# Linear attention and a token/channel mixer on one core: the first batch by halves of the heads, weight loads in another form, attention steps in other slots

## The chip, the core and the metric

The kernel runs on one core of one Trainium2 chip. A core has a matrix engine (TensorE, PE in the profile; PEld is its weight load), a vector engine (VectorE, DVE), an activation engine (ScalarE, ACT), GpSimd (POOL), and SyncE (SP), which here only issues transfers. DVE and ACT read and write both the on-chip memory SBUF and the accumulators of TensorE, PSUM (eight banks of 512 f32 columns for each of 128 partitions); POOL reads and writes SBUF alone. Transfers between HBM and SBUF, and transposes from SBUF to SBUF, are carried by 16 DMA engines. They are issued from SP, ACT or POOL; each issuing engine has a queue of its own, which works in order.

The metric is the device time of one launch in microseconds, the median of several runs. A profiled execution gives the trace; its span is the time from the first to the last instruction.

## The reference

```python
batch, n_heads, seq, head_dim = (8, 8, 576, 64)      # q, k, v in f32
theta = np.pi / 2.0 * pos / S
def phi(x, c, s):
    r = np.maximum(x, 0.0)
    return np.concatenate([r * c, r * s], axis=-1)
q_p = phi(q, cos_w, sin_w); k_p = phi(k, cos_w, sin_w)
kv = np.einsum('bhsf,bhsd->bhfd', k_p, v)
z = np.sum(k_p, axis=2)
num = np.einsum('bhsf,bhfd->bhsd', q_p, kv)
den = np.einsum('bhsf,bhf->bhs', q_p, z)[..., None] + 1e-06
x = (num / den)                                      # then heads side by side: (8, 576, 512)
xt = x.transpose(0, 2, 1)
h = np.maximum(xt @ w_tok1, 0.0) @ w_tok2            # 576 -> 256 -> 576, over tokens
u = x + h.transpose(0, 2, 1)
h2 = np.maximum(u @ w_ch1, 0.0) @ w_ch2              # 512 -> 1536 -> 512, over channels
out = u + h2
```

For each of the 8 batches there is a linear attention over 8 heads, then an MLP over the tokens with a residual, then an MLP over the channels with a residual. The last one holds most of the matrix work.

## The kernel before

The 576 tokens of a batch are laid out over 128 partitions as four full tiles of 128 tokens (j = 0 to 3) and a tail of 64 (j = 4). The tail of an even and of an odd batch use different partitions, so that the tails of two batches form one tile later. Matmuls take bf16 and accumulate in f32.

The steps for a batch b, by the names and lines that the profile gives:

- `load` (L124): q, k and v, two transfers each, into `raw[n][b % 2]` in f32.
- `kfeat`, `qfeat` (L128 to L143): the features, cos half and sin half, one instruction of 128x512 each for a tile; with ACT at L131, with DVE at L133. `vcast` (L145) casts v to bf16.
- `qturn_dma` (L152) or `qturn_pe` (L156): q's features transposed, `qpT`, by a DMA transpose issued from SP or by eight matmuls against the identity and a copy.
- `kv` (L169): eight matmuls of 65 columns a tile, added up over the five tiles in one PSUM tile; `kv_out` (L179) copies them to `kv_sb`.
- `num` (L190): eight matmuls of 65 columns a tile; `x_out` (L198): the denominator, its reciprocal and the product, on DVE, give x in bf16.
- `b1` (L210): the first token matmul, twice five matmuls of 512 columns; `b1_out`: the maximum with 0, to `B1`.
- `u_mm` (L228) for two pairs of tiles, four matmuls each; `u_out` (L237) adds x, in f32; `u_cast` (L241) casts to bf16; `uturn_dma` (L248) or `uturn_pe` (L253) transposes it to `uT`.
- `tail_mm`, `tail_out` (L264, L275): the same for the tails of two batches, once in every odd batch.
- `mlp1` (L287): 12 steps of four matmuls of 512 columns, w_ch1 against `uT`; `mlp1_out` puts the result to `h1T`, with ACT or every third time DVE. `mlp2` (L301): 12 steps of four, h1T against w_ch2; `mlp2_out` (L306) adds u and stores.

The order is written out by hand: each engine runs its instructions in the order of the program text. What stands before L427 is the head: batch 0 up to `uT`, the features and q transposes of batch 1, and the loads of batches 0 to 2. POOL issues the weight loads (L369 to L383), which convert f32 to bf16 on the way. Then the main loop runs over g = 0 to 8. Group g is the channel MLP of batch g (group 8: that of the collected tails) in 24 slots: 12 of `mlp1`, 12 of `mlp2`. Into these slots the attention and token steps of batch b = g + 1 are put (kv in slots 0 to 4, num in 6 to 10, b1 in 12 and 13, u in 15 and 16, the tail in 17), and the features of batch f = g + 2 (k and v in slots 7 to 11, q in 13 to 21 with the DMA transposes). The loads of batch g + 3 are issued from SP when a group begins, behind the transposes of the group before.

PSUM holds four tiles of one bank for the MLP (`psM`) and two of two banks for all else (`psA`), each used in turn.

Of the kernel before, what the change touches and what calls it, by code (L numbers as in the profile page):

```python
# [18 lines left out]
def kernel(  # L19
# [34 lines left out]
    psum = ctx.enter_context(tc.tile_pool(name="psum", bufs=1, space=bass.MemoryType.PSUM))  # L54
# [9 lines left out]
    w2n = sb("w_tok2n", [P, NT, S], BF16)  # L64
# [23 lines left out]
    res = [sb(f"res{i}", [P, 2, Dm], F32) for i in range(2)]  # L88

    psM = [psum.tile([P, 512], F32, name=f"psM{i}") for i in range(4)]  # L90
    psA = [psum.tile([P, 2, 512], F32, name=f"psA{i}") for i in range(2)]
    cnt = {"M": 0, "A": 0}

    def nextM():
        cnt["M"] += 1
        return psM[cnt["M"] % 4]
# [4 lines left out]

    def bf(ps):

        return ps
# [10 lines left out]
    def load(b, src, name, engs):  # L115
# [19 lines left out]
    def kfeat(b, j, e0, e1):  # L135
        src = raw["k"][b % 2][:, :, place(b, j), :]
        feat(e0, kp[j][:, :, 0, :], src, cos_t, j)
        feat(e1, kp[j][:, :, 1, :], src, sin_t, j)

    def qfeat(b, j, e0, e1):  # L140
        src = raw["q"][b % 2][:, :, place(b, j), :]
        feat(e0, qp[j][:, :, 0, :], src, cos_t, j)
        feat(e1, qp[j][:, :, 1, :], src, sin_t, j)  # L143

    def vcast(b, j, eng):  # L145
        src = raw["v"][b % 2][:, :, place(b, j), :]
        if eng is nc.scalar:
            eng.copy(vb[j][:, :, 0:D], src)
        else:
            eng.tensor_copy(vb[j][:, :, 0:D], src)  # L150
# [5 lines left out]
    def qturn_pe(b, j, eng):  # L156
# [4 lines left out]
        if eng is nc.scalar:  # L161
            eng.copy(qpT[:, :, j, :], t)
        else:
            eng.tensor_copy(qpT[:, :, j, :], t)
# [88 lines left out]
    def uturn_pe(b, c, eng):  # L253
# [4 lines left out]
        dst = uT[b % 2][:, 2 * c:2 * c + 2, :, :].rearrange("p t c k -> p (t c) k")  # L258
        if eng is nc.scalar:
            eng.copy(dst, t)  # L260
        else:
            eng.tensor_copy(dst, t)
# [58 lines left out]

    ctx.enter_context(tc.manual_schedule())

    PE_Q = 2
    PE_U = 1

    def loads(b, engs):
        for n, src in (("k", k), ("v", v), ("q", q)):
            load(b, src, n, engs)

    for n, eng in (("k", nc.vector), ("v", nc.vector), ("q", nc.gpsimd)):
        eng.memset(raw[n][0][:, :, 4, :], 0.0)
    loads(0, (nc.sync, nc.scalar))
    for n, eng in (("k", nc.vector), ("v", nc.vector), ("q", nc.gpsimd)):
        eng.memset(raw[n][1][:, :, 0, :], 0.0)


    make_identity(nc, ident)
    pos_i = sb("pos_i", [P, 1], I32)
    nc.gpsimd.iota(pos_i, pattern=[[0, 1]], base=0, channel_multiplier=1)  # L340
    odd_i = sb("odd_i", [P, 1], I32)
    nc.vector.tensor_single_scalar(odd_i, pos_i, 1, op=ALU.bitwise_and)
    pf = sb("pf", [P, 2], F32)
    nc.vector.tensor_copy(pf[:, 0:1], pos_i)
    nc.vector.tensor_copy(pf[:, 1:2], odd_i)

    base = sb("base", [P, 2], F32)
    nc.vector.tensor_scalar(base[:, 0:1], pf[:, 0:1], scalar1=4.5, scalar2=None, op0=ALU.mult)
    half = sb("half", [P, 2], F32)
    nc.vector.tensor_scalar(half[:, 0:1], pf[:, 1:2], scalar1=0.5, scalar2=None, op0=ALU.mult)  # L350
    nc.vector.tensor_scalar(half[:, 1:2], pf[:, 1:2], scalar1=-4.5, scalar2=4.0, op0=ALU.mult, op1=ALU.add)
    tok = sb("tok", [P, NJ], F32)
    nc.vector.tensor_add(base[:, 1:2], base[:, 0:1], half[:, 0:1])
    for j in range(T):
        nc.vector.tensor_scalar_add(tok[:, j:j + 1], base[:, 1:2], float(j))
    nc.vector.tensor_add(tok[:, T:T + 1], base[:, 0:1], half[:, 1:2])
    sc = (math.pi / 2.0) / S
    hp = sb("hp", [P, 1], F32)
    nc.vector.memset(hp, math.pi / 2.0)
    nc.scalar.activation(sin_t, tok, AF.Sin, bias=0.0, scale=sc)  # L360
    nc.scalar.activation(cos_t, tok, AF.Sin, bias=hp, scale=-sc)

    for j in range(NJ):
        nc.gpsimd.memset(vb[j][:, :, D:E1], 1.0)
    nc.gpsimd.memset(w2t, 0.0)
# [4 lines left out]
    nc.gpsimd.dma_start(out=w1[1:P:2, 0:4, :], in_=a[:, 5:9, :])  # L370
    nc.gpsimd.dma_start(out=w1[0:P:2, 4, :], in_=a[:, 4, :])
    nc.gpsimd.dma_start(out=w1[1:P:2, 4, :], in_=a[:, 4, :])
    nc.gpsimd.dma_start(out=w2n, in_=moe_w_tok2.rearrange("(c p) s -> p c s", p=P))

    loads(1, (nc.sync, nc.sync))

    for c in range(4):
        w = D_ch // 4
        nc.gpsimd.dma_start(out=wc1[:, :, c * w:(c + 1) * w],
# [27 lines left out]
    for j in range(NJ):  # L407
        num(0, j)
        x_out(0, j)
# [100 lines left out]
```

## Time and profile before

| what | us |
|---|---|
| median of 3 runs (lowest, highest) | 322.48 (321.37, 324.3) |
| profiled execution: its time | 325.71 |
| profiled execution: its span | 323.8 |
| TensorE busy with matmuls | 264.1 |
| VectorE busy | 154.4 |
| ScalarE busy | 132.0 |
| GpSimd busy | 42.4 |

In the profile, a group of instructions has a line of the kernel, an engine, an operation, its output and input tiles, and then busy time and mean nanoseconds of one, and the idle time of the engine ahead of them with what ended it. In the order of time, a row has start, duration, engine, line, operation and count, and in brackets the idle time before it and its releaser. Matmuls overlap: a row of four 512-column matmuls that lasts 1.02 us may be followed by the next row after 0.86 us, so what matters is the distance between starts. A row of stages has the stretch, its length, busy time and count of PE, PEld, DVE, ACT and POOL, the clock granted to TensorE as a share of full speed, and the busy share and rate of the DMA engines. The granted clock over the whole span was 0.989.

### The profile page before, as it was taken

What the parts mean: (1) busy time and instruction counts of PE and PEld (TensorE: products, weight loads), DVE (VectorE), ACT (ScalarE), POOL (GpSimd) and SP (SyncE); (2) the same over time, 40 slices, a digit from 0 to 9 for tenths busy, and PEclk for the clock granted to TensorE, in tenths of its full rate; (3) what the DMA queues carried; (4) which work ended last, traced back from release to release, by engine and by line L of the source; (5) the groups of instructions that cost most, each with busy time, mean ns of one, the idle gap of its engine ahead of it and who ended that gap; (6) DMA issues with size and microseconds to landing.
All of it is one profiled execution on the core that took longest, in us unless ns stands there. A gap on an engine that the chain in (4) does not pass through costs nothing.

```text
span 323.8 us, 4680 instructions
## 1 busy us (share of the span) xinstructions
PE 264.1 (82%) x1760; PEld 132.2 (41%) x1760; DVE 154.4 (48%) x320; ACT 132.0 (41%) x205; POOL 42.4 (13%) x76
## 2 busy tenths in 40 slices
PE   0144506699979997999799879998997999999994
PEld 0133302455435443544354335444543554444441
DVE  4242641429643861587266606761864365222221
ACT  3344072246435552555273517363743423220410
POOL 9540300020203001130210020303000010000000
PEclk9999999999999997999999979999999999999999
DMA  7999999700299749955995899278019502501102
GB/s 227 289 269 258 253 321 356 244 2 1 39 244 269 263 101 240 290 169 129 230 311 168 155 253 355 42 158 185 1 34 204 120 3 49 161 2 65 65 34 98
DMA packets 81495, 53.89 MB, mean 166 GB/s; under 512 B 50240, under 2 KB 78784, under 8 KB 81472
## 3 DMA queue, kind: packets, MB, share of 16 engines
q1 hardware_dynamic: 72720, 38.94, 47.1%
q10 hardware_dynamic: 4464, 10.88, 10.3%
q0 software_dynamic: 4288, 3.77, 7.1%
q8 instruction: 14, 0.23, 0.3%
q14 instruction: 9, 0.07, 0.1%
HBM read 35.85 MB, written 9.44 MB: 140 GB/s over the span
## 4 chain that ended last, share of the span: by engine, by line
PE 54%; DMA 20%; DVE 16%; ACT 4%; issue 3%; SPq 1%; ACTq 1%; DVEq 0%
PE psM L291 22%; PE psM L303 17%; DMA uT<-u_bf 9%; DMA q_raw<-in_q_dram 7%; PE psA L234 5%; PE psA L216 4%; DVE x_sb L206 4%; DMA v_raw<-in_v_dram 4%; PE psA L174 3%; DVE kp L133 3%; DVE rden L203 2%; DVE u_sb L239 2%; DVE x_tl L206 1%; SPq L124 1%; DVE rden L202 1%
## 5 line engine op out<-in xcount | busy, mean ns | idle before, releaser
L291 PE MATMUL psM<-uT,w_ch 128*128 128x512 bf16 x384 | 98.1, 386 | 13.1 <-DMA uT<-u_bf 13.1
L303 PE MATMUL psM<-w_ch,h1T 128*128 128x512 bf16 x432 | 99.9, 379 | 0.0
L297 ACT ACTIVATE h1T<-psM 128x512 bf16<-128x512 f32 x72 | 42.8, 597 | 80.5 <-PE psM L291 76.7
L303 PEld LDWEIGHTS <-h1T 128*128 128x128 bf16 x432 | 42.2, 98 | 53.6 <-issue 3.3
L291 PEld LDWEIGHTS <-w_ch 128*128 128x128 bf16 x432 | 37.3, 98 | 50.1 <-issue 9.5
L299 DVE TENSOR_SCALAR h1T<-psM 128x512 bf16<-128x512 f32 x36 | 24.8, 688 | 68.2 <-PE psM L291 68.2
L150 POOL CAST vb<-v_raw 128x512 bf16<-128x512 f32 x35 | 22.2, 645 | 148.7 <-PE psA L174 93.8
L308 DVE TENSOR_TENSOR res<-psM,u_sb 128x512 f32<-128x512 f32 x32 | 22.1, 689 | 34.0 <-PE psM L303 34.0
L131 ACT ACTIVATE qp<-q_raw,sin_t 128x512 bf16<-128x512 f32 x40 | 27.2, 713 | 17.9 <-DMA q_raw<-in_q_dram 12.1
L174 PE MATMUL psA<-vb,kp 128*128 128x65 bf16 x320 | 17.8, 203 | 15.5 <-DVE vb L150 15.2
L244 ACT CAST u_bf<-u_sb 128x1024 bf16<-128x1024 f32 x16 | 16.7, 1045 | 27.3 <-DVE u_sb L239 21.6
L131 ACT ACTIVATE kp<-k_raw,sin_t 128x512 bf16<-128x512 f32 x40 | 27.1, 711 | 1.9 <-DMA k_raw<-in_k_dram 1.9
L239 DVE TENSOR_TENSOR u_sb<-psA,x_sb 128x1024 f32<-128x1024 f32 x16 | 19.6, 1224 | 16.3 <-PE psA L234 15.7
L216 PE MATMUL psA<-x_sb,w_tok 128*128 128x512 bf16 x64 | 18.1, 409 | 10.4 <-ACT B L222 10.0
L174 PEld LDWEIGHTS <-kp 128*128 128x128 bf16 x320 | 16.2, 104 | 24.9 <-issue 16.0
L133 DVE TENSOR_SCALAR qp<-q_raw,cos_t 128x512 bf16<-128x512 f32 x40 | 19.5, 505 | 6.7 <-DMA q_raw<-in_q_dram 6.7
L206 DVE TENSOR_TENSOR x_sb<-psA,rden 128x512 bf16<-128x512 f32 x32 | 22.1, 691 | 1.1
L133 DVE TENSOR_SCALAR kp<-k_raw,cos_t 128x512 bf16<-128x512 f32 x40 | 20.2, 508 | 3.2 <-DMA k_raw<-in_k_dram 3.2
L194 PEld LDWEIGHTS <-qpT 128*128 128x128 bf16 x320 | 15.8, 102 | 10.4 <-issue 2.1
L222 ACT ACTIVATE B<-psA 128x512 bf16<-128x512 f32 x16 | 9.5, 596 | 23.9 <-PE psA L216 23.9
L194 PE MATMUL psA<-kv_sb,qpT 128*128 128x65 bf16 x320 | 17.3, 199 | 1.7 <-DVE x_sb L206 1.3
L234 PE MATMUL psA<-B,w_tok 128*128 128x512 bf16 x64 | 18.4, 410 | 0.3 <-ACT B L222 0.3
(61 smaller groups left out, 130.0 us busy)
## 6 DMA issues: line engine op xcount, KB each, us to landing
out_dram<-res ACTq DMA_DIRECT2D x32, 256.0 KB, 3.3
k_raw<-in_k_dram SPq DMA_DIRECT2D x7, 640.0 KB, 7.2
v_raw<-in_v_dram SPq DMA_DIRECT2D x7, 640.0 KB, 9.0
q_raw<-in_q_dram SPq DMA_DIRECT2D x7, 640.0 KB, 10.1
k_raw<-in_k_dram SPq DMA_DIRECT2D x8, 512.0 KB, 5.1
v_raw<-in_v_dram SPq DMA_DIRECT2D x8, 512.0 KB, 8.6
q_raw<-in_q_dram SPq DMA_DIRECT2D x8, 512.0 KB, 9.5
w_ch<-in_moe_w_ch_dram POOLq DMA_DIRECT2D x4, 384.0 KB, 18.7
```

Source lines behind the costliest of these rows:

```text
L131: eng.activation(out_ap, in_ap, AF.Relu, bias=0.0, scale=s)
L133: eng.tensor_scalar(out_ap, in_ap, scalar1=s, scalar2=0.0, op0=ALU.mult, op1=ALU.max)
L174: nc.tensor.matmul(ps[:, h // HH, (h % HH) * E1:(h % HH + 1) * E1], kp[j][:, h, :, :].rearrange("p a d -> p (a d)"), vb[j][:, h, 0:E1], st ...
L194: nc.tensor.matmul(ps[:, h // HH, (h % HH) * E1:(h % HH + 1) * E1], qpT[:, h, j, :], kv_sb[:, h, 0:E1], start=True, stop=True, skip_group_ ...
L206: nc.vector.tensor_mul(dst.rearrange("p (g h d) -> p g h d", g=2, h=HH), n[:, :, :, 0:D], rb)
L216: nc.tensor.matmul(ps[:, mi, :], w1[:, j, mi * P:(mi + 1) * P], rhs, start=(j == 0), stop=(j == NJ - 1))
L234: nc.tensor.matmul(ps[:, half, :], w2[:, ki, 2 * c + half, :], B1[b % 2][:, ki, :], start=(ki == 0), stop=(ki == NT - 1))
L239: nc.vector.tensor_add(u_sb[b % 2][:, 2 * c:2 * c + 2, :], ps, x_sb[:, 2 * c:2 * c + 2, :])
L291: nc.tensor.matmul(ps.rearrange("p (t k) -> p t k", k=P), wc1[:, ki, mi * P:(mi + 1) * P], src[:, :, ki, :], start=(ki == 0), stop=(ki == ...
L297: eng.activation(h1T[:, mi, :], ps, AF.Relu)
L299: eng.tensor_relu(h1T[:, mi, :], ps)
L303: nc.tensor.matmul(ps, h1T[:, ki, t * P:(t + 1) * P], wc2[:, ki, :], start=(ki == 0), stop=(ki == NCH - 1))
```

## The change

- **Head.** Batch 0 is loaded, and worked on, by halves of the heads (four heads each): features, transposes, kv, num, x and the first token matmul for half A, then for half B. It uses a PSUM pool of its own (`psN`, `psK`, `psT`), which is given back before the main tiles are made. `uT` of batch 0 is no longer the transpose of a cast u: TensorE adds the transposed x (a matmul against the identity) and the transposed token MLP in one bank for each 128 channels (`uT_x`, `uT_h`), and a copy gives `uT`. u itself, in f32 for the residual, is computed in slots 1 and 3 of group 0. Twelve and eight matmuls on zeros (`warm`) are put in.
- **Weights.** They are loaded in f32 on SP's queue, behind the halves of batch 0 and ahead of batch 1, in the order in which they are needed, into buffers that are not yet in use (`h1T`, `res`, `u_sb[1]`, `u_tl`); POOL, and ACT for four slices of w_ch2, casts them to bf16. The second and third part of w_ch2 are issued from ACT.
- **Group 0** is written out: its MLP, with all of batch 1's features, q transposes (on TensorE), kv, num, b1 and u in it. Its `mlp2` runs by parts over the four tiles.
- **Group 1** has the whole attention of batch 2 and the tail step of batch 1 in it.
- **Groups 2 to 8**: num in slots 2 to 6, b1 in 8 and 9, u in 11 and 12, the tail in 13; kv of batch f in slots 18 to 22, so a group earlier than before; q's features in 12 to 20. Loads of batch 2 and later are issued from POOL; from batch 4 on behind a one-column copy on POOL (`load_late`) that reads the latest evacuated tile.

The core of the diff:

```diff
-    res = [sb(f"res{i}", [P, 2, Dm], F32) for i in range(2)]
-    psM = [psum.tile([P, 512], F32, name=f"psM{i}") for i in range(4)]
-    psA = [psum.tile([P, 2, 512], F32, name=f"psA{i}") for i in range(2)]
+    res_all = sb("res", [P, 2, 2, Dm], F32)
+    res = [res_all[:, i] for i in range(2)]
+    wz = sb("wz", [P, 512], BF16)
...
+    psN = [hp_.tile([P, 2, 512], F32, name=f"psN{i}") for i in range(2)]
+    psK = [hp_.tile([P, 512], F32, name=f"psK{i}") for i in range(2)]
+    psT = [hp_.tile([P, 512], F32, name=f"psT{i}") for i in range(2)]
...
+    def uT_x(c, bank):
+        for t in range(T):
+            nc.tensor.matmul(bank[:, t * P:(t + 1) * P], x_sb[:, t, c * P:(c + 1) * P], ident,
+                             start=(t == 0), stop=False, skip_group_check=True)
+    def uT_h(b, c, bank):
+        for ki in range(NT):
+            nc.tensor.matmul(bank, B1[b % 2][:, ki, c * P:(c + 1) * P],
+                             w2[:, ki, :, :].rearrange("p t k -> p (t k)"),
+                             start=False, stop=(ki == NT - 1), skip_group_check=True)
...
-    loads(0, (nc.sync, nc.scalar))
+    for n in "kqv":
+        load(0, src_of[n], n, (A if n != "v" else SY, SY), 0, HH)
...
+    for n in "kqv":
+        load(0, src_of[n], n, (SY, SY), HH, H)
...
-    nc.gpsimd.dma_start(out=w1[0:P:2, 0:4, :], in_=a[:, 0:4, :])
+    SY.dma_start(out=st_w1[0:P:2, 0:4, :], in_=a[:, 0:4, :])
...
-    nc.gpsimd.dma_start(out=w2n, in_=moe_w_tok2.rearrange("(c p) s -> p c s", p=P))
-    loads(1, (nc.sync, nc.sync))
+    SY.dma_start(out=st_w2, in_=moe_w_tok2.rearrange("(c p) s -> p c s", p=P))
...
-        nc.gpsimd.dma_start(out=wc1[:, :, c * w:(c + 1) * w],
-                            in_=moe_w_ch1[:, c * w:(c + 1) * w].rearrange("(c p) m -> p c m", p=P))
+    SY.dma_start(out=wc1_st[0][:, :, 0:256], in_=wc1_src[:, :, 0:256])
+    SY.dma_start(out=wc1_st[0][:, :, 256:512], in_=wc1_src[:, :, 256:512])
+    SY.dma_start(out=wc1_st[1], in_=wc1_src[:, :, 512:1024])
+    SY.dma_start(out=wc1_st[2], in_=wc1_src[:, :, 1024:1536])
...
+    warm(12)
+    for j in range(NJ):
+        f1("k", j, 0, V, CA)
+        f1("k", j, 1, A, CA)
+    for j in range(NJ):
+        f1("q", j, 0, V, CA)
+        f1("q", j, 1, A if j < 3 else V, CA)
...
+    head.__exit__(None, None, None)
+    psum = ctx.enter_context(tc.tile_pool(name="psum", bufs=1, space=bass.MemoryType.PSUM, reuse_waits="tile"))
+    psA += [psum.tile([P, 2, 512], F32, name=f"psA{i}") for i in range(2)]
+    psM += [psum.tile([P, 512], F32, name=f"psM{i}") for i in range(4)]
+    wc2_load(0, SY)
+    for n in "kqv":
+        load(1, src_of[n], n, (SY, SY))
+    for mi in range(NCH):
+        if mi in (1, 3):
+            u_mm(0, mi // 2)
+        ps = mlp1(0, mi)
+        mlp1_out(mi, ps, V if mi % 3 == 2 else A)
+        if mi in (1, 3):
+            u_out(0, mi // 2)
+        if mi < 8:
+            wc1_cast(4 + mi, G)
+        if mi >= 7:
+            kfeat(1, mi - 7, V, A)
+        if mi >= 10:
+            wc2_load(mi - 9, A)
+        if mi in (2, 3):
+            w2t_perm(mi - 2, G)
+    for ki in range(4):
+        wc2_cast(ki, G)
+    mps = [nextM() for _ in range(4)]
+    for j in range(NJ):
+        qfeat(1, j, V, A if j < 3 else V)
+    for j in range(NJ):
+        vcast(1, j, G)
+    for j in range(NJ):
+        if j < 4:
+            mlp2(0, j, 0, mps[j])
+        if j == 2:
+            for i in range(NJ):
+                kv(1, i)
+            kv_out(1, A)
+        tq[j] = qturn_mm(j)
+        qturn_out(j, tq[j], (V, A)[j % 2])
+    for ki in range(4, 12):
+        wc2_cast(ki, G if ki < 8 else A)
+    for n in "kqv":
+        load(2, src_of[n], n, (G, G))
+    for j in range(NJ):
+        num(1, j)
+        x_out(1, j)
+        if j:
+            mlp2(0, j - 1, 1, mps[j - 1])
...
+    def load_late(b):
+        if last_out[0] is not None:
+            G.tensor_copy(late, last_out[0])
+        for n in "kqv":
+            load(b, src_of[n], n, (G, G))
...
+        if g == 1:
+            put(0, lambda: G.tensor_add(x_tc, x_tl[0], x_tl[1]))
+            put(2, tail_step, 1)
+            for j in range(NJ):
+                put(j, kfeat, b, j, V, A)
+                put(j + 1, q_step, b, j)
+                put(j + 3, vcast, b, j, G)
+                put(j + 4, kv_step, b, j)
+                put(j + 9, num_step, b, j)
+            for n in range(2):
+                put(14 + n, b1_step, b, n)
+                put(16 + n, u_step, b, n)
+            put(5, lambda: [load(3, src_of[n], n, (G, G)) for n in "kqv"])
+            put(19, load_late, 4)
+            for j in range(NJ):
+                put(11 + j, k_step, f, j)
+                put(12 + j, q_step, f, j)
+                put(18 + j, kv_step, f, j)
+            return plan
+        if g + 3 < B:
+            put(4 if g == 2 else 0, load_late, g + 3)
+        if b < B:
+            for j in range(NJ):
+                put(2 + j, num_step, b, j)
+            for n in range(2):
+                put(8 + n, b1_step, b, n)
+                put(11 + n, u_step, b, n)
+            put(13, tail_step, b)
+        if f < B:
+            for j in range(NJ):
+                put(7 + j, k_step, f, j)
+                put(12 + 2 * j, q_step, f, j)
+                put(18 + j, kv_step, f, j)
+        return plan
...
-        if g + 3 < B:
-            loads(g + 3, (nc.sync, nc.sync))
...
-            if b < B:
-                if s < 5:
-                    kv(b, s)
-                    if s == 4:
-                        kv_out(b, A)
-                elif 6 <= s < 11:
-                    num(b, s - 6)
-                    x_out(b, s - 6)
```

More of the change, by code (lines that the diff above doesn't have):

```diff
@@ L95, in nextM @@
         cnt["M"] += 1
-        return psM[cnt["M"] % 4]
+        return psM[(cnt["M"] - 1) % 4]
     def nextA():
@@ L357 @@
+    V.tensor_add(tok[:, T:T + 1], base[:, 0:1], half[:, 1:2])
     sc = (math.pi / 2.0) / S
     hp = sb("hp", [P, 1], F32)
[L359 to L361 removed]
+    V.memset(hp, math.pi / 2.0)
+    A.activation(sin_t, tok, AF.Sin, bias=0.0, scale=sc)
+    A.activation(cos_t, tok, AF.Sin, bias=hp, scale=-sc)
+    make_identity(nc, ident)
     for j in range(NJ):
[L364 removed]
@@ new lines, in warm, with f1, turn @@
+    def warm(n):
+        for _ in range(n):
+            nc.tensor.matmul(psK[1], wz[:, 0:P], wz, start=True, stop=True)
+    pairs = ((0, 1), (2, 3), (4,))
+    num_b = {0: psN[0], 1: psN[1], 2: psN[0]}
+    CA, CB = (0, HH), (HH, H)
+    def f1(n, j, which, eng, hs):
+        src = raw[n][0][:, hs[0]:hs[1], place(0, j), :]
+        dst = (kp if n == "k" else qp)[j][:, hs[0]:hs[1], which, :]
+        feat(eng, dst, src, (cos_t, sin_t)[which], j)
+    def turn(hf, i):
+        turn_half(hf, pairs[i], psT[i % 2])
```

379 lines of the change are left out of this document (265 added, 114 removed).

## The prediction

> **What bounds the kernel now.** I read the span by stage first, then TensorE's waits, then the order of time on each engine in the first 66 us, then DMA. By stage (microseconds; busy time and count of each engine, granted clock, DMA share, GB/s): the time before the first channel-MLP matmul, then group 4, 6, 7 and 8 of the main loop.
>
> ```profile
> 0.00:65.36 65.36, 24.57 (x194) 16.17 (x195) 25.12 (x64) 22.42 (x34) 18.02 (x42) 1.00 1.03 275
> ...
> 188.07:220.11 32.04, 29.62 (x198) 14.46 (x199) 18.02 (x36) 15.36 (x24) 4.66 (x6) 0.95 0.76 204
> ...
> 249.96:278.07 28.11, 28.07 (x199) 13.89 (x199) 12.73 (x26) 9.18 (x14) 1.15 (x1) 1.00 0.37 82
> 278.07:298.96 20.89, 20.89 (x97) 9.52 (x98) 5.53 (x8) 4.67 (x8) 0.00 (x0) 1.00 0.14 54
> 298.96:323.80 24.84, 20.72 (x97) 9.17 (x94) 6.22 (x9) 4.67 (x8) 0.00 (x0) 1.00 0.17 64
> ```
>
> A fifth of the span goes by before the MLP starts, with TensorE busy 24.57 of 65.36 us. After that TensorE is the bound: group 7 is nothing but 96 matmuls in 20.89 us. TensorE's longest waits:
>
> ```profile
> PE psA L174 <- DVE vb L150: 15.2, 2, 14.7
> PE psM L291 <- DMA uT<-u_bf: 13.1, 6, 3.0
> PE psA L216 <- ACT B L222: 10.0, 1, 10.0
> ```
>
> The first and third lie in the head, the second is one wait at the start of each of groups 1 to 6. The third is no slow ScalarE:
>
> ```profile
> 5.07 0.28 ACT L361 ACTIVATE cos_t<-tok,hp 128x5 f32<-128x5 f32 x1
> ...
> 28.64 1.01 ACT L162 COPY qpT<-psA 128x1024 bf16<-128x1024 bf16 x1 [2.80 <-PE psA L160]
> ...
> 42.39 0.72 ACT L131 ACTIVATE qp<-q_raw,sin_t 128x512 bf16<-128x512 f32 x1 [11.51 <-DMA q_raw<-in_q_dram]
> 43.02 0.71 ACT L131 ACTIVATE kp<-k_raw,sin_t 128x512 bf16<-128x512 f32 x1
> ```
>
> At 42.39 ScalarE had stood 11.51 us for batch 1's q; batch 0's B1, which the chain needs, is queued behind all nine features of batch 1. TensorE in the head, then in the steady loop, then at the start of group 4:
>
> ```profile
> 17.68 0.60 PE L174 MATMUL psA<-vb,kp 128*128 128x65 bf16 x8 [0.52 <-DVE vb L150]
> 20.25 1.03 PE L160 MATMUL psA<-ident,qp 128*128 128x128 bf16 x8 [1.97 <-ACT qp L131]
> ...
> 48.54 1.86 PE L216 MATMUL psA<-x_sb,w_tok 128*128 128x512 bf16 x4 [9.96 <-ACT B L222]
> ...
> 64.42 1.16 PE L160 MATMUL psA<-ident,qp 128*128 128x128 bf16 x16 [0.25 <-ACT qpT L162]
> ```
>
> ```profile
> 102.97 0.41 PE L194 MATMUL psA<-kv_sb,qpT 128*128 128x65 bf16 x8
> 103.22 1.02 PE L291 MATMUL psM<-uT,w_ch 128*128 128x512 bf16 x4
> 104.08 0.41 PE L194 MATMUL psA<-kv_sb,qpT 128*128 128x65 bf16 x8
> ```
>
> ```profile
> 188.07 1.89 PE L291 MATMUL psM<-uT,w_ch 128*128 128x512 bf16 x4 [3.05 <-DMA uT<-u_bf]
> ```
>
> From start to start, a step of eight short matmuls costs 0.25 us (103.22 - 102.97) and four 512-wide ones 0.86, 0.216 each. After a long idle the same four take 1.86 to 1.89, twice as much: about 0.43 each.
>
> **Price of the main loop.** TensorE's work in a group: MLP 96 x 0.216 = 20.74; b1 10 x 0.216 = 2.16; u 8 x 0.216 = 1.73; five kv and five num steps 2.5; tail 0.86 in groups with odd batch. That is 27.1, or 28.0 with tail. Group 6 runs at its price (28.11); groups 0 to 6 together take 278.07 - 65.36 = 212.7 against 4 x 28.0 + 3 x 27.1 = 193.3: **19.4 us** of stalls, 13.1 of them the named wait on uT, the rest mostly half-rate matmuls behind it.
>
> **The change, part by part.**
>
> *Plans of groups 2 to 6.* u moves from slots 15, 16 to 11, 12, so its transposes are issued about four slots (over 4 us) earlier and no longer between those of q. The longest wait was 3.05: it goes. kv moves one group ahead, the same work elsewhere. Loads leave SP for POOL, so SP holds transposes alone. POOL takes six issues per batch:
>
> ```profile
> L150 POOL CAST vb<-v_raw 128x512 bf16<-128x512 f32 x35 | 22.2, 645 | 148.7 <-PE psA L174 93.8 <-issue 42.0 <-DVE rden L203 12.9
> ...
> L379 POOL DMA_DIRECT2D w_ch<-in_moe_w_ch_dram x4 | 3.0, 782 | 1.3 <-DMA w_tok<-in_moe_w_tok_dram 1.3
> ```
>
> 6 x 0.78 = 4.7 us, plus five casts 3.2 and a small copy that waits for the previous evacuation: 8 of 27 us, hidden. Behind the waiting copy stand only casts due at slot 7. Groups 2 to 6 cost 28.0 + 27.1 + 28.0 + 27.1 + 26.7 (group 6 has no kv left; 28.0 - 1.25) = 136.9. The wait of b1 for the last x falls too; I leave 1.5 us for what remains: **138.4** (bounds 136.9, all gone; 156, all 19 back).
>
> *Head.* Rates of pure f32 loading (45 to 60 us) and of loading mixed with POOL's converting weight loads (22 to 34):
>
> ```profile
> 22.00:34.00 12.00, 5.73 (x56) 4.66 (x57) 4.74 (x13) 4.48 (x6) 1.55 (x3) 1.00 1.19 256
> 45.00:60.00 15.00, 6.90 (x21) 2.39 (x20) 4.17 (x6) 5.74 (x9) 0.00 (x0) 1.00 1.08 360
> ```
>
> A batch is 3 x 8 x 576 x 64 x 4 B = 3.54 MB. At 360 GB/s from 2.5 us: half A lands at 7.4, half B at 12.3, w_tok1 and w_tok2 (1.18 MB) at 15.6, the first 256 columns of w_ch1 at 17, all of it (3.15 MB) at 24.4. The durations of DVE:
>
> ```profile
> 26.97 0.87 DVE L133 TENSOR_SCALAR qp<-q_raw,cos_t 128x512 bf16<-128x512 f32 x2
> 31.40 0.69 DVE L164 COPY qpT<-psA 128x1024 bf16<-128x1024 bf16 x1 [3.56 <-PE psA L160]
> 32.01 0.16 DVE L202 TENSOR_SCALAR rden<-psA 128x8 f32<-128x8 f32 x1
> 32.20 0.20 DVE L203 RECIPROCAL rden<-rden 128x8 f32<-128x8 f32 x1
> 32.44 0.69 DVE L206 TENSOR_TENSOR x_sb<-psA,rden 128x512 bf16<-128x512 f32 x1
> ```
>
> A half-width feature I estimate at 0.27 on DVE (0.43 a full one) and 0.39 on ACT (0.63 from start to start above). Tables stand at 5.35. Half A: features to 8.7; transposes (1.03 per eight) and copies (0.69 and 1.01) to 11.3; kv to 12.3, its copy 12.7. Half B: features, DVE to 15.1 and ACT to 15.8; meanwhile num 1.0 and eight warming matmuls at 0.43 end at 16.8; transposes and ACT's copy 18.5; kv and copies 20.0; num 20.6; x in stages 22.6, last chunk 23.4; b1 and B1 25.2; the uT sums (0.43 each) 26.3; copies 27.0. Some ten hand-overs at 0.15 that I did not count add 1.5: **28.5** instead of 65.36. POOL must have cast by then: 8 half v casts, w1, w2 and four w_ch1 slices end near 24 at 0.65 each, so it hides. Lower bound 25 (the last third of w_ch1 lands at 24.4), upper 34 (half-rate TensorE throughout, 3; POOL's permutes at twice my price, 2.5).
>
> *Group 0, with batch 1 inside.* 56 matmuls (w_ch1 and u) 12.1, two slots and two turns 3: TensorE stands before kv at 43.5. v of batch 1 is behind 12.45 MB: 37.1, and with the 2.1 MB of w_ch2 on ACT's ring up to 43; I take 41. Five POOL casts (3.2): kv starts at 44.5. Then kv 1.25, its copy 0.6, three turns through two PSUM tiles 3, five num steps at DVE's pace 5.2 (0.16 + 0.20 + 0.69 each), B1 and b1 2.8, MLP 3.5, u 1.73, two turns 1.2, copy 1.0, first evacuation 0.7: 65.5, and 1 for hand-overs: **38** us, to 66.5. TensorE's own work in it is 33 (lower bound); the weight casts (12 x 0.65 = 7.8 on POOL, four on ACT) hide under it. The upper bound is a rival below. SP's and ACT's issues of these loads stand before nothing that is due earlier.
>
> *Group 1.* Work: 28.0 + 1.25 (both kv) = 29.2. All of batch 2's attention lies in one group. Its five q transposes share the DMA engines with the load of batch 3, its uT transposes with that of batch 4.
>
> ```profile
> 184.67 5.44 SPq L153 DMA_TRANSPOSE qpT<-qp  x3
> ```
>
> At 1.8 each they need 9 us, at half speed beside a load 18, begun at 1.5: done at 10.5 or 19.5, due at slot 13, 14.3. So 0 to 5; u's second transpose, issued near 24 and due at 29.2, is 0 to 3 late. I take 4, the middle of 0 to 8: **33.2**.
>
> *Sum.* 28.5 + 38 + 33.2 + 138.4 + 20.9 + 24.8 = 283.8 of span (before: 323.8). The profiled execution was 325.71, 1.9 more than its span: 285.7. It ran 1.0% above the median of 322.48, so **283** in terms of the median.
>
> **A rule weighed.** A 9.96 us gap is followed by half-rate matmuls, sixteen transposes at 64.42 run at 0.07 each instead of 0.13; a 3.05 us gap cools it too. The eight warming matmuls should thus hold full rate to the end of the head, whose gaps stay under 2; at half rate b1 and the uT sums would cost 3 us more. The Trainium skill ("TensorE: Matmul & The Clock Gate", Part 1) says the array's clock halves after an idle window of about 3.4 us and comes back after as much sustained work. By that rule the head is 28.5, without it 31.5; the trace agrees in kind, its 3.05 us being a little under the rule's window.
>
> **Rivals.**
> 1. *Batch 1 arrives late.* With two rings in use the rate was 256, not 360: 12.45 MB land at 51, kv starts at 54.3, 10 us later: 293. For it: the ring also waits for POOL's casts before w_ch2's first part. Against: one ring, no converting loads.
> 2. *The stalls come back elsewhere*, as transposes beside POOL's loads or evacuations queued behind features on ACT: up to the 19.4 us again, 301. Against: ACT is busy 15.36 of 32 us in group 4.
> 3. *POOL's loads are too slow* (slower than before). Queue q0 is POOL's:
>
> ```profile
> q0 software_dynamic: 4288, 3.77, 7.1%
> ```
>
> 0.071 x 16 x 323.8 / 4288 = 86 ns of engine time a packet; a batch has 3072, so 16.5 us, in a group of 27. It decides only where six batches lose the 39.5 us gained (322.5 - 283), 6.6 each, at 33.6 us a load, twice that; at 34.5 it gives 283 + 6 x 7.5 = 328. POOL does slow beside DVE:
>
> ```profile
> 17.19 0.61 POOL L389 COPY w_tok<-w_tok2n 128x128 bf16<-128x128 bf16 x1
> 17.75 0.41 POOL L390 COPY w_tok<-w_tok2n 128x128 bf16<-128x128 bf16 x1
> ```
>
> The same copy takes 0.61 while DVE works and 0.41 after it: 1.5 times, which makes 7 us of the issues, still hidden. The Trainium skill ("DMA: Bandwidth & Descriptors", SWDGE vs HWDGE vs iDMA) gives this rival its mechanism: descriptors of such loads are written by GpSimd, which VectorE's two-port modes lock out. No run here shows it on a load.
> 4. *Group 0 and 1 run at TensorE's own price* (33 and 29.2): 274.
>
> **How the numbers follow.** The forecast's case has 0.62, rivals 1 to 4 have 0.16, 0.12, 0.03 and 0.07. Range 272 to 299: from rival 4 with a head 2 us shorter, through rival 1 with the later head (299); it leaves out rivals 2 and 3, 0.15. Within 1% is what a measurement here cannot tell from no change; only a mix near rival 3 ends there, 0.01. Faster 0.96, slower 0.03.
>
> **What would show it.** First w_ch1 matmul at 26 to 31 us, at 0.216 spacing; kv of batch 1 near 44; group 1 from 64 to 69 us; no wait of w_ch1 matmuls on uT in groups 3 to 7; q transposes of batch 2 as TensorE's wait in group 1. I am wrong in the head if POOL's casts or DVE's half features end last there, in group 0 if v lands after 45, in the loop if any group from 2 to 6 is over 29.5.

## The result, and the profile after

| what | us |
|---|---|
| median before, in the same comparison (lowest, highest) | 322.56 (321.37, 324.3) |
| median after (lowest, highest) | 303.83 (303.22, 306.13) |
| profiled execution after: its time, its span | 303.22, 301.2 |

The ratio of after to before is 0.9429, 95% interval 0.9362 to 0.9495. The change is faster, by about half of what was forecast: 283 was predicted, and 303.83 lies above the range of 272 to 299. The ratios here and below leave out executions in a slower state, two of them (306.67 and 306.84) of the four of run 6 and one (297.66) of run 5. By stage of the kernel after (start and end, length, busy time and count of PE, PEld, DVE, ACT and POOL, granted clock, DMA share, GB/s): the head, groups 0, 1, 2, then 6, 7 and 8.

```profile
0.00:24.08 24.08, 18.04 (x182) 10.93 (x185) 15.97 (x67) 14.75 (x29) 13.97 (x40) 1.00 0.94 331
24.08:61.93 37.85, 32.67 (x254) 17.36 (x258) 23.17 (x43) 17.86 (x27) 20.80 (x34) 1.00 0.80 273
61.93:113.03 51.10, 30.78 (x235) 14.87 (x239) 23.48 (x49) 21.36 (x35) 11.03 (x18) 0.88 0.90 243
113.03:143.53 30.50, 30.34 (x195) 14.63 (x199) 17.78 (x35) 15.12 (x24) 8.97 (x13) 0.91 0.64 169
...
227.88:255.17 27.29, 26.92 (x158) 12.79 (x159) 13.23 (x26) 8.36 (x13) 1.15 (x1) 1.00 0.44 94
255.17:275.89 20.72, 20.67 (x96) 9.41 (x96) 5.53 (x8) 4.67 (x8) 0.00 (x0) 1.00 0.12 51
275.89:301.20 25.31, 20.67 (x95) 9.17 (x94) 6.23 (x9) 4.67 (x8) 0.00 (x0) 0.96 0.16 63
```

Against the sum of the prediction:

| stage | predicted | measured | difference |
|---|---|---|---|
| head | 28.5 | 24.08 | -4.4 |
| group 0 | 38 | 37.85 | -0.2 |
| group 1 | 33.2 | 51.10 | +17.9 |
| groups 2 to 6 (113.03 to 255.17) | 138.4 | 142.14 | +3.7 |
| groups 7 and 8 | 45.7 | 46.03 | +0.3 |
| span | 283.8 | 301.2 | +17.4 |

One stage holds the miss. TensorE's longest waits after (what waited, what it waited for, us in total, times, longest), and TensorE in the order of time at the end of group 1:

```profile
PE psM L286 <- DMA uT<-u_bf: 14.8, 1, 14.8
PE psA L190 <- DMA qpT<-qp: 4.5, 4, 2.2
PE psM L286 <- ACT h1T L292: 2.2, 4, 1.1
```

```profile
97.19 1.02 PE L298 MATMUL psM<-w_ch,h1T 128*128 128x512 bf16 x4
113.03 5.30 PE L286 MATMUL psM<-uT,w_ch 128*128 128x512 bf16 x12 [14.81 <-DMA uT<-u_bf]
...
118.46 1.02 PE L286 MATMUL psM<-uT,w_ch 128*128 128x512 bf16 x4
```

The six short waits on `uT` are gone, and one of 14.8 us has come, with twelve matmuls at 0.44 behind it (5.30 / 12) that in groups 3 to 6 take 2.75. What SP's queue and then POOL did just before:

```profile
92.47 1.23 SPq L245 DMA_TRANSPOSE uT<-u_bf  x1
93.86 1.41 SPq L149 DMA_TRANSPOSE qpT<-qp  x1
95.31 3.73 SPq L245 DMA_TRANSPOSE uT<-u_bf  x1
```

```profile
93.75 0.19 POOL L712 COPY late<-res 128x1 f32<-128x1 f32 x1 [13.73 <-DVE res L303]
93.98 1.37 POOL L119 DMA_DIRECT2D k_raw<-in_k_dram  x2
95.34 1.37 POOL L119 DMA_DIRECT2D q_raw<-in_q_dram  x2
96.70 1.37 POOL L119 DMA_DIRECT2D v_raw<-in_v_dram  x2
```

POOL's load of batch 4 is issued from 94 us on, and its packets move from 97 to 112, so the second transpose of u, issued at 95.31, meets nearly all of it. That transpose landed 17.7 us after its issue, where the median of those of `uT` is 2.7. The DMA queues (packets, MB, busy time as a share of 16 engines) in the stretch from 98 to 104 us, where q0 carries POOL's load, q10 ACT's output stores and q1 SP's transposes, and then from 78 to 85 us, where transposes of q are alone:

```profile
q0 software_dynamic: 324, 1.33, 80.2%
q10 hardware_dynamic: 82, 0.27, 12.3%
q1 hardware_dynamic: 337, 0.08, 7.2%
```

```profile
q1 hardware_dynamic: 3699, 0.91, 68.3%
```

The two queues get about one packet each (324 and 337 in 6 us), but a packet of the load has 1.33 MB / 324 = 4.1 KB and one of the transpose about 250 B. So the transpose gets 7.2% of the engines' time, 56 packets a microsecond, where transposes alone reached 3699 / 7 = 528. Turns of one packet each give about that: a packet of the load keeps an engine for 238 ns (80.2% of 16 x 6 us, by 324) and one of the transpose for 21 (7.2%, by 337), so 16 engines make an estimated 16 / 0.259 = 62 of each a microsecond. The transpose goes on at a tenth of its pace until the load is done. Two of the load's issues (0.69 us each) make one row of 1.37, so POOL itself was not slow.

### The profile page after: what moved, and what is told of

The parts are those of the page before. It is cut to its first block, busy times and chain, and to the rows that moved or that the text cites. A ratio compares the mean times of both kernels' runs of the same rounds, so it can differ in the third digit from the quotient of the medians.

```text
span 301.2 us, 4824 instructions
## 1 busy us (share of the span) xinstructions
PE 261.9 (87%) x1789; PEld 130.2 (43%) x1814; DVE 156.6 (52%) x341; ACT 131.0 (43%) x214; POOL 75.3 (25%) x134
## 4 chain that ended last, share of the span: by engine, by line
PE 67%; DMA 16%; DVE 8%; ACT 4%; issue 2%; SPq 2%; DVEq 0%; ACTq 0%
PE psM L298 27%; PE psM L286 23%; DMA qpT<-qp 8%; DMA uT<-u_bf 6%; PE psA L212 5%; PE psA L230 5%; PE psA L170 2%; DVE qp L127 2%; DMA k_raw<-in_k_dram 2%; PE psA L190 2%; SPq L149 1%; DVE kp L127 1%; DVE res L303 1%; PE psA L266 1%; ACT kp L125 1%
## 5 line engine op out<-in xcount | busy, mean ns | idle before, releaser
L286 PE MATMUL psM<-uT,w_ch 128*128 128x512 bf16 x384 | 94.2, 387 | 18.6 <-DMA uT<-u_bf 14.8
L286 PEld LDWEIGHTS <-w_ch 128*128 128x128 bf16 x432 | 40.5, 99 | 64.5 <-DMA uT<-u_bf 15.3
L294 DVE TENSOR_SCALAR h1T<-psM 128x512 bf16<-128x512 f32 x36 | 24.7, 686 | 23.9 <-PE psM L286 18.5
L143 POOL CAST vb<-v_raw 128x512 bf16<-128x512 f32 (+1 forms) x43 | 25.9, 638 | 44.2 <-DMA v_raw<-in_v_dram 32.9
L125 ACT ACTIVATE kp<-k_raw,sin_t 128x512 bf16<-128x512 f32 (+1 forms) x45 | 29.1, 668 | 5.5 <-DVE kp L127 4.2
L235 DVE TENSOR_TENSOR u_sb<-psA,x_sb 128x1024 f32<-128x1024 f32 x16 | 19.5, 1221 | 19.8 <-PE psA L230 19.6
L125 ACT ACTIVATE qp<-q_raw,sin_t 128x512 bf16<-128x512 f32 (+1 forms) x39 | 25.1, 683 | 7.7 <-DVE qp L127 7.6
L127 DVE TENSOR_SCALAR kp<-k_raw,cos_t 128x512 bf16<-128x512 f32 (+1 forms) x45 | 22.2, 526 | 1.9 <-DMA k_raw<-in_k_dram 1.9
L198 DVE TENSOR_SCALAR rden<-psA 128x8 f32<-128x8 f32 x35 | 5.6, 159 | 32.5 <-PE psA L190 32.0
L127 DVE TENSOR_SCALAR qp<-q_raw,cos_t 128x512 bf16<-128x512 f32 (+1 forms) x45 | 19.8, 469 | 0.8 <-DMA q_raw<-in_q_dram 0.8
L202 DVE TENSOR_TENSOR x_sb<-psA,rden 128x512 bf16<-128x512 f32 x28 | 19.4, 691 | 1.0
L230 PE MATMUL psA<-B,w_tok 128*128 128x512 bf16 x64 | 16.4, 379 | 0.3 <-DVE B L220 0.3
L170 PEld LDWEIGHTS <-kp 128*128 128x128 bf16 x280 | 12.6, 98 | 8.9 <-DVE qpT L143 1.8
L170 PE MATMUL psA<-vb,kp 128*128 128x65 bf16 x280 | 13.6, 193 | 1.3 <-DVE qpT L143 1.3
```

Of the source, the lines that this page charges most:

```text
L125: eng.activation(out_ap, in_ap, AF.Relu, bias=0.0, scale=s)
L127: eng.tensor_scalar(out_ap, in_ap, scalar1=s, scalar2=0.0, op0=ALU.mult, op1=ALU.max)
L143: eng.tensor_copy(out_ap, in_ap)
L170: nc.tensor.matmul(ps[:, h // HH, (h % HH) * E1:(h % HH + 1) * E1], kp[j][:, h, :, :].rearrange("p a d -> p (a d)"), vb[j][:, h, 0:E1], st ...
L230: nc.tensor.matmul(ps[:, half, :], w2[:, ki, 2 * c + half, :], B1[b % 2][:, ki, :], start=(ki == 0), stop=(ki == NT - 1))
L235: nc.vector.tensor_add(u_sb[b % 2][:, 2 * c:2 * c + 2, :], ps, x_sb[:, 2 * c:2 * c + 2, :])
```

## The experiments

Ratios are to the kernel before, with 95% intervals.

**1. Load of batch 4 behind the transposes of u.** The gate on POOL reads what those transposes write.

```diff
-            put(19, load_late, 4)
+            def load_gated():
+                G.tensor_copy(late, uT[0][:, 3, NCC - 1, P - 1:P])
+                load_late(4)
+            put(19, load_gated)
```

> Edit: batch 4's load, issued by POOL in slot 19 of group 1, first waits until batch 2's second uT transpose has landed. The changed kernel is at 303.8, with a wait of 14.8 us of the first w_ch1 matmul of group 2 on uT and twelve half-rate matmuls behind it (2.6 us). Theory 1 (DMA engines take turns between queues packet by packet, so 256-byte transpose packets crawl beside POOL's 4096-byte load packets): the wait falls to 2 us or less, the half-rate matmuls go, about 287. Theory 2 (the transpose is late because five q transposes stand ahead of it on SP): the wait stays above 8 us, 298 to 304.

307.0 us, ratio 0.9459 (0.9371 to 0.9548). The wait on `uT` fell from 14.8 to 1.5 us and group 2 began at 101.07 instead of 113.03, with no half-rate matmuls; the total did not move. TensorE in group 3 of this kernel shows where the 12 us went (it waited 7.09 and 6.05 us for q's transposes):

```profile
141.19 0.62 PE L190 MATMUL psA<-kv_sb,qpT 128*128 128x65 bf16 x8 [7.09 <-DMA qpT<-qp]
...
149.57 0.62 PE L190 MATMUL psA<-kv_sb,qpT 128*128 128x65 bf16 x8 [6.05 <-DMA qpT<-qp]
```

The waits on `qpT` are 19.5 us in all, from 4.5. The next loads now met the q transposes of batch 4, four of which held SP from 127.79 for 18.05 us. The stall is not tied to u: it comes wherever a transpose and a load from POOL meet, and the order on SP, which this kernel leaves as it was, is not its cause.

**2. Load of batch 4 from ACT's queue, at the same place, with no gate.**

```diff
-            put(19, load_late, 4)
+            put(19, lambda: [load(4, src_of[n], n, (A, A)) for n in "kqv"])
```

> Edit: the same load in the same slot, not gated, but issued from ACT's queue, whose packets are 1024 to 1280 bytes. Theory 1 (turns by packet): 64 packets of a transpose on each DMA engine, each beside one of about 50 ns in place of 182, make about 5 us a transpose; the last uT transpose lands before the load's end, the wait is 3 to 6 us, about 293. Theory 1b (a transpose stands still while any load of another queue is under way): it lands with the load's end near 106, wait 8 us, 297. Theory 2 (order on SP): 14 us, 303.

310.56 us in a single execution. The wait on `uT` is 4.8 us and its longest landing 7.7, against 14.8 and 17.7, with the same bytes at the same place in packets of 1 KB to 1.3 KB instead of 4.1. That the smaller packets are the reason is not shown by it, because the two queues seldom moved at once: from 99 to 101 us ACT's queue moved 298 packets and SP's 104, from 101 to 103 it was 302 and 926. The transpose went mostly while ACT's load paused. ACT in the order of time shows what a load costs on that engine:

```profile
96.50 2.17 ACTq L119 DMA_DIRECT2D k_raw<-in_k_dram  x2
98.71 1.56 ACTq L119 DMA_DIRECT2D q_raw<-in_q_dram  x2
101.21 2.62 ACTq L119 DMA_DIRECT2D v_raw<-in_v_dram  x2
103.93 0.60 ACT L180 CAST kv_sb<-psA 128x520 bf16<-128x520 f32 x1 [8.14 <-issue]
```

For 8.14 us ACT did nothing but issue this load and two output stores, and the copy of kv, whose matmuls had ended at 98.98, stood behind them until 103.93. Later a load from POOL met five q transposes, with one wait of 13.95 us on `qpT`. So the total says nothing of the load's price at this place; the landing time does.

**3. No warming matmuls.** `warm(12)` and `warm(8)` are taken out.

> Edit: the 12 and the 8 warming matmuls on zeros are left out. If the head's chain runs through TensorE at full rate, as the prediction had it: half-rate transposes, b1 and uT sums, the first w_ch1 matmul moves from 24.1 to about 27, 306 to 307. Rival, the head is bound by features, copies and landings: within 1 us of 303.8, or up to 1 us earlier, as the eight matmuls stand ahead of half B's transposes.

304.22 us, ratio 0.9376 (0.9311 to 0.9442), so no change of the total. The first w_ch1 matmul:

```profile
25.33 1.02 PE L286 MATMUL psM<-uT,w_ch 128*128 128x512 bf16 x4 [0.24 <-ACT uT L141]
```

It comes 1.25 us later than with them (24.08), and group 1 begins at 64.24 instead of 61.93. Of these 2.3 us 1.7 are left at the start of group 2 (114.70 for 113.03, behind a wait on `uT` of now 15.7) and 0.6 at that of group 3 (144.16 for 143.53): the first num waits 0.8 us for q's transposes instead of 2.2, and the twelve matmuls behind the long wait take 4.31 instead of 5.30. Nor is the 1.25 us sure to be the warming's: kernels of other runs, whose head has it unchanged, reach that matmul between 23.82 (run 4) and 25.55 (run 10), and in run 10 the granted clock was 0.50 from 9.0 to 12.4 us in spite of it.

**4. The old slots for num, b1, u and the tail in groups 2 to 6.** All else is the kernel after.

```diff
-                put(2 + j, num_step, b, j)
+                put(6 + j, num_step, b, j)
             for n in range(2):
-                put(8 + n, b1_step, b, n)
-                put(11 + n, u_step, b, n)
-            put(13, tail_step, b)
+                put(12 + n, b1_step, b, n)
+                put(15 + n, u_step, b, n)
+            put(17, tail_step, b)
```

> Edit: in groups 2 to 6 num, b1, u and the tail go back to their old slots (6 to 10, 12 and 13, 15 and 16, 17); loads stay on POOL, kv stays a group ahead. If the new slots took the uT waits away: a wait of 2 to 3 us and half-rate matmuls return at the starts of groups 3 to 7, 312 to 318. Rival, that the loads left SP's queue did it: under 305.5.

303.35 us, ratio 0.9365 (0.9296 to 0.9434). TensorE's wait on `uT` in this kernel:

```profile
PE psM L286 <- DMA uT<-u_bf: 16.1, 2, 15.6
```

15.6 of it is the wait of group 2; in all later groups together it is 0.5, with u in the slots where the kernel before waited some 2 us in every group. The earlier slots are not what removed those waits. Two other parts of the change remain for that, the loads that left SP's queue and kv a group earlier; these runs do not separate them.

**5. Loads of batches 3 to 7 from SP.** The slots stay, without the gate on POOL.

```diff
-            G.tensor_copy(late, last_out[0])
+            pass
         for n in "kqv":
-            load(b, src_of[n], n, (G, G))
+            load(b, src_of[n], n, (SY, SY))
...
-            put(5, lambda: [load(3, src_of[n], n, (G, G)) for n in "kqv"])
+            put(5, lambda: [load(3, src_of[n], n, (SY, SY)) for n in "kqv"])
```

> Edit: loads of batches 3 to 7 in the same slots, issued from SP, without the gating copy; so they stand in one queue with the transposes, behind those issued earlier. After the last run the theory reads: load packets of another queue take turns with the 256-byte packets of transposes, and the wait appears at whichever transposes a load meets (uT in the changed kernel, qpT of batch 4 when batch 4's load was gated). Then in one queue no transpose is slowed by a load behind it: uT wait of group 2 under 2, qpT waits under 3, about 286 (283 to 291). Rival: transposes standing behind loads in one queue wait as long as they did beside them: 298 or more, with uT or qpT waits over 8 us.

295.23 us, ratio 0.9108 (0.9026 to 0.919): 8.6 us better than the change, by the queue and the gate that fell with it, but short of the 286 expected. Waits on `uT` 3.3 us, on `qpT` 2.4, and the longest landing of `uT` 4.3. On SP's queue transpose and load stand one behind the other. What is missing to 286 lies in group 1, which still takes 42.47 us (61.73 to 104.20). Batch 3's k now stands behind the transposes and comes late, and an MLP evacuation is queued behind its feature on DVE:

```profile
82.37 0.49 DVE L127 TENSOR_SCALAR kp<-k_raw,cos_t 128x512 bf16<-128x512 f32 x1 [3.47 <-DMA k_raw<-in_k_dram]
82.78 0.68 DVE L294 TENSOR_SCALAR h1T<-psM 128x512 bf16<-128x512 f32 x1
```

TensorE waited 2.9 us for that evacuation and 1.7 for the last x, and from 84.5 to 92 us its granted clock was 0.50.

**6. POOL's loads, kept apart from the transposes.** Load 3 right behind load 2, load 4 gated on the turn of u, loads 5 to 7 a group later and gated on the last turn of q.

```diff
+    for b_ in (2, 3):
         for n in "kqv":
-            load(2, src_of[n], n, (G, G))
+            load(b_, src_of[n], n, (G, G))
...
-            put(19, load_late, 4)
+            def load_uT():
+                G.tensor_copy(late, uT[0][:, 3, NCC - 1, P - 1:P])
+                load_late(4)
+            put(19, load_uT)
...
-        if g + 3 < B:
-            put(4 if g == 2 else 0, load_late, g + 3)
+        def load_qT(nb):
+            G.tensor_copy(late, qpT[:, H - 1, NJ - 1, P - 1:P])
+            load_late(nb)
+        if 3 <= g and g + 2 < B:
+            put(0, load_qT, g + 2)
```

> Edit: loads stay on POOL but are kept clear of transposes: batch 3's is issued right behind batch 2's, batch 4's waits for the uT transposes of batch 2, those of batches 5 to 7 start a group later (slot 0 of groups 3 to 5) and wait for the last q transpose. Theory: uT and qpT waits together under 5 us, group 1 near 34, about 283 (280 to 288). Rival (loads now come too late): kfeat at slot 7 waits for k and evacuations behind it stall TensorE 2 us or more in groups 3 to 5, above 289.

304.52 us (300.68 to 306.84), ratio 0.9337 (0.925 to 0.9424). The collisions are gone (`uT` 1.6, `qpT` 0.2 us), and a new wait has come, of the token matmuls on B, 12.8 us in three groups. ACT in group 3:

```profile
133.14 0.60 ACT L292 ACTIVATE h1T<-psM 128x512 bf16<-128x512 f32 x1 [1.60 <-PE psM L286]
139.61 0.72 ACT L125 ACTIVATE kp<-k_raw,sin_t 128x512 bf16<-128x512 f32 x1 [5.88 <-DMA k_raw<-in_k_dram]
140.24 0.58 ACT L292 ACTIVATE h1T<-psM 128x512 bf16<-128x512 f32 x1
140.72 0.59 ACT L218 ACTIVATE B<-psA 128x512 bf16<-128x512 f32 x1
```

The feature of k stood 5.88 us for a load that now comes late, and the MLP's evacuation and B's are queued behind it. It is the same picture as in the head of the kernel before.

**7. The same places, but loads 4 to 7 from SP and without gates.** The order of SP's queue keeps them behind the transposes.

> Edit: as the run before, but batches 4 to 7 are loaded from SP without gates: behind the transposes in one queue. Theory: as the run before or up to 2 us better, as no gate's reply is waited for: 281 (278 to 287).

287.41 us, ratio 0.8918 (0.8848 to 0.8987). Waits on B 3.6, on `uT` 1.7, on `qpT` 0.5 us: what is left is the late k again.

**8. The kernel before, with its loop's loads from POOL and nothing else changed.**

```diff
-            loads(g + 3, (nc.sync, nc.sync))
+            loads(g + 3, (nc.gpsimd, nc.gpsimd))
```

> Edit, in the kernel before: the loads in the main loop are issued from POOL in place of SP, nothing else. A load for group g then starts in slot 21 of the group ahead, when the buffer comes free, beside the last transposes. Theory (turns by packet): the waits on uT at the starts of groups 1 to 4 grow from 2 to 3 us to 8 to 15 each, 345 to 375. Rival (the queue is of no account): 318 to 326.

400.03 us in a single execution, 77 more than the kernel before, and more than expected. TensorE's wait on `uT` and the landing of those transposes, in this kernel; before they were 13.1 us in six waits, and 2.7, 4.0 and 5.6:

```profile
PE psM L291 <- DMA uT<-u_bf: 79.1, 6, 25.0
```

```profile
DMA to landing us min/median/max: 2.7/7.3/29.3
```

This one line, without any other part of the change, makes the stall, and in four groups instead of one (25.0, 16.0, 16.4 and 17.5 us): there POOL's load is in flight whenever u is turned, and also beside q's transposes that stand ahead of u's on SP (the one at 97.19 held SP for 12.09 us). In the kernel after it is so in group 1 alone.

**9 and 10. The k features of groups 2 to 5 behind B's evacuation**, in the kernels of runs 7 (loads from SP) and 6 (loads from POOL):

```diff
-                put(7 + j, k_step, f, j)
+                put(10 + j, k_step, f, j)
```

> As the run with loads 4 to 7 issued from SP behind the q transposes, and the k features and v casts of groups 2 to 5 in slots 10 to 14 where they stood in 7 to 11. Theory: the three waits of the token matmuls on B (3.6 us) come from k features that stand ahead of B's evacuation on ACT and wait for their load; behind it they hold up nothing, so that wait is under 0.5 us and the median 284 (281 to 286). Rival: ACT itself is too full there, the wait moves to kv in slots 18 to 22 or to the q transposes, and the median stays at 286 to 290.

> The same move of the k features in the kernel whose loads 4 to 7 are issued from POOL, each gated on the transposes it would meet. Theory: a load from POOL costs only by whom it meets and by being late; with both taken away the wait on B falls from 12.8 to under 2 us, the waits on transposes stay under 2, and the median is 287 (284 to 292), within 5 us of the same kernel with SP's loads. Rival: POOL's loads cost something by themselves (their issue, the casts behind them on POOL), and the median stays above 296.

With SP 284.46 us (283.37 to 285.11), ratio 0.8785 (0.8737 to 0.8833); with POOL 286.39 (283.1 to 287.1), ratio 0.8859 (0.8806 to 0.8911). No wait on B is left among the longest in either. Both beat both kernels. The same loads from POOL that cost 77 us in run 8 cost at most a few when they meet no transpose and come before they are needed. Groups 1, 2, 3 and 6 of run 9, and group 1 of run 10:

```profile
63.82:98.70 34.88, 30.32 (x239) 15.25 (x239) 23.58 (x49) 21.33 (x35) 3.52 (x5) 1.00 0.79 176
98.70:126.61 27.91, 27.91 (x198) 13.96 (x199) 16.72 (x35) 15.22 (x24) 4.17 (x6) 1.00 0.82 211
126.61:153.66 27.05, 27.05 (x196) 13.60 (x195) 17.62 (x35) 14.59 (x23) 3.67 (x5) 1.00 0.88 237
208.60:235.28 26.68, 26.68 (x159) 12.74 (x158) 13.14 (x26) 8.36 (x13) 1.15 (x1) 1.00 0.45 90
```

```profile
62.69:97.65 34.96, 30.34 (x238) 15.26 (x239) 22.89 (x49) 21.33 (x35) 3.85 (x7) 1.00 0.87 198
```

In groups 2, 3 and 6 TensorE is busy for the whole of the group: the loop stands at its price.

## Why the prediction was right and wrong

**Wrong: group 1, "at half speed beside a load".** This is the step that failed. It priced a transpose beside a load as if each got half of the engines' time, and allowed u's second transpose "0 to 3 late". In the long wait the two queues moved about equal numbers of packets (324 and 337), and POOL's is sixteen times the size of the transpose's, so the transpose had 7.2% of the engines' time and not half. TensorE waited 14.8 us for it, and its clock stayed at half for 5.3 us more. That the meeting with POOL's load makes the stall is shown by taking it away (runs 1 and 9) and by making it (run 8); that the size of the packets sets its length agrees with the counts, but no run here changes the size alone. With the meetings taken away (run 9) group 1 is 34.88 long, 1.7 over its 33.2; so 16.2 of the 17.9 us were the meetings, 13.2 of them the wait on `uT` (14.81 for 1.63). The q transposes of batch 2, which the prediction feared more, were a small part: beside the load of batch 3 the first of them took 10.6 us to land, and the first num, at 77.85, waited 2.2 us for it.

The rule for this was at hand. The Trainium skill ("DMA: Bandwidth & Descriptors", Queues, rings and completion order) says that each DMA engine goes round the queues that have work and takes a whole packet from one before it turns to the next. The 324 and 337 packets agree with it. The prediction used the same page for another mechanism, descriptors of POOL's loads held up by VectorE: the issues took 0.69 us each in a loop in which VectorE is busy half of the time, and loads from POOL came as fast as those from SP once apart from transposes (medians to landing of the larger transfers of k, q and v: 5.5, 8.5 and 10.4 us in run 10, for 6.7, 9.2 and 10.1 from SP in run 9). Rival 3 has nothing for it here.

**Wrong: "Loads leave SP for POOL, so SP holds transposes alone", taken as a gain without a price.** On SP's queue the loads had been kept in order with the transposes; on another queue they run beside them. Run 5 puts 8.6 us on that move in the kernel after, run 8 puts 77 on it in the kernel before. The prediction looked at POOL's issue time, found it hidden, and it was; the cost lay with the neighbours of the transfer.

**Half right: the second rival, "the stalls come back elsewhere".** It named transposes beside POOL's loads and stood at 301, where the kernel came out. It was given 0.12 and argued down by ACT's idle time, which bears only on its other half, and it placed the stalls in all groups up to a bound of 19.4, where one group holds nearly all.

**Right for a wrong reason: the uT waits of groups 3 to 7.** They went, as forecast, but not because u "moves from slots 15, 16 to 11, 12": with the old slots they are gone too (run 4).

**Right in size: group 0, the loop, groups 7 and 8.** Group 0 took 37.85 for 38, partly by chance. v of batch 1 landed at 38.5, 2.5 before the time taken for it and far from the 51 of the first rival; but kv began 18.3 us after the group's start instead of 16, and what follows kv took 19.6 instead of 22. Groups 2 to 6 took 3.7 more than 138.4; 2.5 of that are the cold matmuls behind the long wait (5.30 - 2.75). Once the meetings are gone they take 136.58 (98.70 to 235.28), against the 136.9 of their price.

**Mis-sized: the head, 24.08 for 28.5.** TensorE after, in the head:

```profile
1.74 4.69 PE L512 MATMUL psK<-wz 128*128 128x512 bf16 x12 [1.74 <-DVE wz L427]
...
12.65 1.67 PE L512 MATMUL psK<-wz 128*128 128x512 bf16 x7
14.35 0.80 PE L331 MATMUL psT<-ident,qp 128*128 128x128 bf16 x8
...
15.50 0.77 PE L342 MATMUL psK<-vb,kp 128*128 128x65 bf16 x20
...
17.82 0.42 PE L355 MATMUL psN<-kv_sb,qpT 128*128 128x65 bf16 x8 [0.64 <-ACT qpT L141]
```

The half features came about as estimated: those of half B end at 14.3 on DVE and 15.1 on ACT, for 15.1 and 15.8. But kv needs k's features and v alone, not q's transposes. The working set half B's kv behind the transposes and their copy, with "kv and copies" at 20.0; it ran among the transposes from 15.50, and its copy was done at 16.69, so that num waited for ACT's copy of q alone, done at 17.76 for 18.5. That is 2.2 of the 4.4 us: 1.5 for kv, which was not on the chain, and 0.7 for features and transposes. The last x was done at 20.61 for 23.4, and the 1.5 set aside for hand-overs was not needed. The head came out below even its lower bound of 25. That bound was the landing of the last third of w_ch1; it landed at 25.2, but the first matmul does not read it. The rule that was weighed, a clock that stays up through the head, shows at most the 1.25 us of run 3 and not 3, and even that lies within what the same head varies by. In this execution the first twelve matmuls brought the clock up early, so the second warming went at 0.24 each (1.67 / 7) and not at 0.43. Without any warming (run 3) the head's own matmuls reach full rate by 12.3 us and lose it once more, at a granted clock of 0.50 from 15.5 to 18.8, behind the gap that the second warming fills: half B's kv takes 1.29 us there for 0.77, the transposes behind it 1.47 for 0.83. b1 and the uT sums, whose half rate was to cost the 3 us, ran at full rate without warming too.

**What would have shown it.** Three of the prediction's signs read as named: kv of batch 1 at 42.4 ("near 44"), q transposes as a wait in group 1, no `uT` wait in groups 3 to 7. Two were passed on the early side: the first w_ch1 matmul at 24.08 (26 to 31) and the start of group 1 at 61.93 (64). The sign against it, "any group from 2 to 6 over 29.5", showed in group 2 (30.50). No sign was named for a wait on `uT` at the end of group 1, where the long one stood.

**Open.** With the meetings gone group 1 takes 34.88 for 33.2: in run 9 TensorE is busy there for 30.32 us, for a price of 29.2, and waits 1.9 for ACT's evacuations, 1.6 for `uT` and 1.0 for x, for the 4 set aside; which of these could go was not tried. Nor was the share of kv's earlier place in the end of the `uT` waits. Run 5, with the loads on SP and the new slots, has one such wait in groups 3 to 7, of 1.79 us.

## What to carry to other kernels

Before a transfer is moved to another queue, price what it will meet there, by the packet sizes of both: here a transpose of small packets went at a tenth of its pace for as long as a load of large ones lasted. Keep transposes and bulk loads in one queue, in the order in which they are due, or apart in time; and then look at what stands in order behind the instruction that consumes the load, since a load moved out of one collision may come late for an engine that holds others' evacuations. A stall that is removed at one meeting and returns whole at the next (run 1) points to the traffic, not to the waiting step.

## What the runs showed of the hardware

- A load issued from POOL went in packets of 4096 B (3.54 MB in 864 packets, run 1); the kernel before, with its loads on SP, moved 6.45 MB in 5727 packets of SP's queue from 44 to 62 us, 1.1 KB each. The prediction had taken 3072 packets a batch for POOL's too.
- Two queues with work got about equal numbers of packets, and so very unequal shares of the engines' time. From 106 to 108 us in the kernel after it was 127 of POOL's to 117 of the transpose, from 108 to 110 it was 177 to 177, and from 72 to 73, with the output stores as a third, 57, 57 and 55 of the transposes. But from 102 to 104 it was 130 to 82, and from 67 to 72 the transposes got 22 packets, all after 70 us, beside 269 of POOL's and 241 of the stores. The trace does not show whether a queue had a packet waiting at such times, so this stays open.
- In the long wait the granted clock fell from 1.00 to 0.50 between 101.2 and 101.3 us, 3.0 us after TensorE's last work (98.21), and was back 5.3 us after the restart at 113.03. In the kernel before it fell at 187.5, 2.5 us after the last work ahead of group 4 (185.02), and was back 2.9 us after the restart at 188.07. So neither delay is a fixed one here. The stretches at half rate lasted 3.41 us in the kernel before (187.54 to 190.95) and 17.07, five times that, in the kernel after (101.24 to 118.31); 13.65 in run 3 (104.21 to 117.87) is four times. In the kernel after:

```profile
101.10:101.20 0.10, 0.00 (x0) 0.00 (x0) 0.00 (x0) 0.00 (x0) 0.00 (x0) 1.00 0.10 41
101.20:101.30 0.10, 0.00 (x0) 0.00 (x0) 0.00 (x0) 0.00 (x0) 0.00 (x0) 0.71 0.00 0
101.70:113.00 11.30, 0.00 (x0) 0.00 (x0) 0.00 (x0) 0.00 (x0) 0.00 (x0) 0.50 0.92 309
```
